# One level of Strassen's identity in the spatial product of a mixer kernel, with intermediates moved through DRAM

## The chip, the cores and the metric

The kernel runs on one core of a Trainium2 chip. The metric is the time of one execution on the device in microseconds (us). The core has a matrix engine (TensorE, PE in the profile, with its weight loads shown apart as PEld), VectorE (DVE), ScalarE (ACT), GpSimd (POOL) and SyncE (SP). PE multiplies a stationary 128x128 block by a moving block and adds into one of eight accumulator banks (PSUM); a bank holds 512 floats in each of 128 partitions. DMAs are issued from the queues of SP, ACT and POOL. Every engine takes its own instructions in the order of its program; engines wait for one another by semaphores.

## What is computed

`x` has 2048 rows (tokens) of 512. Two branches work on the normalized rows and are added to `x`.

```python
xn = layernorm(x)
# A: linear attention, 32 heads of 16
q, k, v = split(xn @ wqkv)
phi(t) = concat(softmax(t @ w_phi), softmax(-(t @ w_phi)))     # per head
o = phi(q) @ (phi(k)^T v) / (phi(q) . sum_s phi(k) + 1e-6)
A = o @ wo
# B: gated MLP, F = 1376, Fh = 688
z = gelu(xn @ w_in);  z1, z2 = z[:, :688], layernorm(z[:, 688:])
g = w_sp @ z2 + b_sp                    # 2048x2048 by 2048x688: the spatial product
B = (z1 * g) @ w_out
out = x + A + B
```

All data is 32-bit. A product that must keep precision is made from two parts of each operand, a rounded one (`h`, type fp32r) and the rest (`l`): h·h + h·l + l·h, three matmuls (`mm3`, L48). `round_h` (L39) makes h, mostly on ACT, and `rest_l` (L45) makes l on DVE.

## The kernel before, in words

The tokens are 16 tiles of 128 rows (`NT`); 688 is taken as two halves of 344 (`FC`). The statements are given in program order, but a scheduler of the framework orders the instructions of each engine by its own estimate of times, so parts of neighbouring stages interleave. Buffers come from pools; a tile that reuses a buffer waits for the last user of it.

**Projections (L145 to L301).** For each tile `s`: `center` subtracts the mean, transposes the tile on PE and splits it into `xT`; `proj_k`, `proj_q` and `proj_v` are 12 matmuls of 512 columns each; `softmax_pair` (L89) makes the two exponentials of k, their sums and reciprocals on DVE (maximum L92, minimum L93, two subtractions L95 and L96, sums L99, reciprocals L101) and ACT (L97). `proj_q` (L241) only scales the product on ACT and stores it to DRAM (`pq_d`). `add_kv` (L247) multiplies the exponentials by the reciprocals (L249), splits the product into kh and kl, adds it into `zacc` by an accumulating DMA on POOL's queue (L255) and adds to `kvps` with three fp32r matmuls of 256 columns for each of four head groups (L259). `z1_raw` (L122) makes the first half of the MLP input for 11 of the 16 tiles in this stage and stores it to DRAM (`z1_d`); the other five follow (L341).

**Second half of the MLP input (L366 to L386).** Per tile 24 matmuls of 344 columns (`zproj`), gelu on ACT, statistics on DVE (L376), the reciprocal deviation on POOL (`rstd_of`, L78), normalization on DVE (L382), and a split into `Z` (h and l) that stays on the chip. `kv_T` (L351) transposes and splits the attention state and broadcasts the sums of phi(k) into `zb`.

**Spatial product, attention and output together (L398 to L562).** For each output tile `i` and each of four quarters `q` of the 16 input tiles: `load_w` fetches a block of w_sp and splits it, two quarters ahead; `spatial` (L411) issues 4 x 6 matmuls of 344 columns into two banks. Around these stand, by hand: `q_prep` (L313), which loads the stored q product, runs `softmax_pair`, and makes phi(q) already divided by its denominator (multiplications by zb L319, sums L320, small operations L321 to L326, final product L328), stored by a DMA on SP's queue into an fp32r tile `er`; `attend` (L449), which for two tiles and one head group transposes er on PE (L454), splits (`fh`, `fl`), multiplies by the state (`po`) and splits again (`oT`); `gate` (L466), z1 times g plus bias; `gate_T` (L477), which transposes the gated tile on PE and splits it (`uh`, `ul`, `rt`); and `project` (L495), 29 matmuls of 512 columns with w_out and wo and the addition of x. So PE has matmuls of `spatial` to issue while the short chains of the other parts run.

Of the kernel before, what the change touches and what calls it, by code (L numbers as in the profile page):

```python
# [18 lines left out]
P = 128  # L19
S, D, H, DH, FH = 2048, 512, 32, 16, 688  # L20
NT = S // P
# [8 lines left out]
XB = 6  # L30
# [3 lines left out]
def mixer(ctx: ExitStack, tc: tile.TileContext, x, x_t, wv, wqkT, phi_bd, wo, w_in, wst, b_r, w_out, out):  # L34
# [4 lines left out]
    def round_h(eng, h, src):  # L39
        if eng is act:  # L40
            act.activation(h, src, AF.Copy)  # L41
        else:
            eng.tensor_copy(h, src)

    def rest_l(l, src, h, eng=None):  # L45
        (eng or dve).tensor_tensor(l, src, h.bitcast(F32), op=ALU.subtract)  # L46
# [14 lines left out]

    cst = ctx.enter_context(left("cst", 1))
    xz = ctx.enter_context(left("xz", NT))
    dram = ctx.enter_context(tc.tile_pool(name="dram", bufs=1, space=DRAM))
    pq_d = dram.tile([NT, P, D], F32, name="pq_d")
    z1_d = dram.tile([NT, P, FH], F32, name="z1_d")

# [21 lines left out]
    def softmax_pair(pl, src, tag, scale=1.0, ebufs=2):  # L89

        mm = pl.tile([P, 2, H], F32, tag=tag + "mm", bufs=2, name="mm")
        dve.tensor_reduce(mm[:, 0], heads(src), axis=AX.X, op=ALU.max)  # L92
        dve.tensor_reduce(mm[:, 1], heads(src), axis=AX.X, op=ALU.min)  # L93
        e = pl.tile([P, NF], F32, tag=tag + "e", bufs=ebufs, name="e")
        dve.tensor_tensor(heads(e[:, :D]), heads(src), bc(mm[:, 0], H), op=ALU.subtract)  # L95
        dve.tensor_tensor(heads(e[:, D:]), bc(mm[:, 1], H), heads(src), op=ALU.subtract)  # L96
        act.activation(e, e, AF.Exp, scale=scale)  # L97
        sm = pl.tile([P, 2 * H], F32, tag=tag + "sm", bufs=2, name="sm")
        dve.tensor_reduce(sm, heads(e), axis=AX.X, op=ALU.add)  # L99
        r = pl.tile([P, 2 * H], F32, tag=tag + "r", bufs=2, name="r")  # L100
        dve.reciprocal(r, sm)  # L101
        return e, r
# [4 lines left out]
    kvps = kv_ps_p.tile([P, NG, 2 * P], F32, name="kvps")  # L107
# [4 lines left out]
    def zproj(ps, s, w):  # L112
        p = ps.tile([P, 2, D], F32, tag="z", name="zps")
        t = xT[s]
        for j in range(2):
            for c in range(ND):
                cs = slice(c * P, (c + 1) * P)
                mm3(p[:, j, :FC], (t[:, 0, cs], t[:, 1, cs]), (w[j][0][:, c], w[j][1][:, c]),
# [19 lines left out]
    ones = w1_pool.tile([P, P], F32R, name="ones")  # L138
    ones_f = w1_pool.tile([P, P], F32, name="ones_f")
    pool.memset(ones_f, 1.0)  # L140
    dve.tensor_copy(ones, ones_f)
# [3 lines left out]
    with ExitStack() as p0:  # L145
# [42 lines left out]
        def load_win(dst, j, stp, bufs):  # L188
            for c in range(ND):
                t = stp.tile([P, D], F32, tag="x", bufs=bufs, name="wst_")  # L190
# [38 lines left out]
        def proj_v(s):  # L229
            pv = proj(s, wv_h, wv_l)  # L230
            vh = wk.tile([P, D], F32R, tag="vh", name="vh")
            vl = wk.tile([P, D], F32R, tag="vl", name="vl")
            r = r_x[:, s:s + 1]
            act.activation(vh, pv, AF.Copy, scale=r)
            dve.scalar_tensor_tensor(vl, pv, r, vh.bitcast(F32), op0=ALU.mult, op1=ALU.subtract)
            v[s] = vh, vl
# [4 lines left out]
        def proj_q(s):  # L241
            pq = proj(s, wqk_h[:, 0], wqk_l[:, 0])
            qs = wk.tile([P, D], F32, tag="qs", bufs=1, name="qs")
            act.activation(qs, pq, AF.Copy, scale=r_x[:, s:s + 1])
            act.dma_start(pq_d[s], qs)

        def add_kv(s, e, rs):  # L247
            vh, vl = v.pop(s)
            dve.tensor_tensor(heads(e), heads(e), bc(rs, 2 * H), op=ALU.mult)  # L249
            kh = wk.tile([P, 2, D], F32R, tag="kh", bufs=1, name="kh")  # L250
            kl = wk.tile([P, 2, D], F32R, tag="kl", bufs=1, name="kl")
            e2 = e.rearrange("p (a b) -> p a b", a=2)
            round_h(act, kh, e2)
            rest_l(kl, e2, kh)
            pool.dma_start(zacc, e, accum_op=ALU.add)  # L255
            for g in range(NG):
                gs = slice(g * P, (g + 1) * P)
                for i, (a, b) in enumerate(((vh, kh), (vh, kl), (vl, kh))):
                    pe.matmul(kvps[:, g], a[:, gs], b[:, :, gs],  # L259
                              start=(s == 0 and i == 0 and g % 2 == 0),  # L260
                              stop=(s == NT - 1 and i == 2), skip_group_check=True)
# [25 lines left out]
        n1 = 0  # L287
        for s in range(NT):
            fetch(s + 4)
            e, rs = ek if s == 0 else proj_k(s)  # L290
            if s + 2 < NT:
                center(s + 2)
            proj_q(s)
            add_kv(s, e, rs)
            if s + 2 < NT:
                proj_v(s + 2)
            if s in (0, 1):
                load_win(w1[s], s, wk, XB)
# [5 lines left out]
    Z = []  # L304
    ws = ctx.enter_context(right("ws", 2))
    cpre = ctx.enter_context(right("cpre", 1))
    kvT_h = cpre.tile([P, 2 * NG, P], F32R, name="kvT_h")
    kvT_l = cpre.tile([P, 2 * NG, P], F32R, name="kvT_l")
    zb = cpre.tile([P, NF], F32, name="zb")
    qp = ctx.enter_context(right("qp", 2))  # L310
    es = {}

    def q_prep(s):  # L313
        pq = qp.tile([P, D], F32, tag="pq", name="pq")
        sp.dma_start(pq, pq_d[s])
        e, r = softmax_pair(qp, pq, "q", ebufs=1)
        t = qp.tile([P, 2 * H], F32, tag="qt", name="qt")
        for a in range(2):
            dve.tensor_tensor(pq, e[:, a * D:(a + 1) * D], zb[:, a * D:(a + 1) * D], op=ALU.mult)  # L319
            dve.tensor_reduce(t[:, a * H:(a + 1) * H], heads(pq), axis=AX.X, op=ALU.add)  # L320
        dve.tensor_tensor(t, t, r, op=ALU.mult)  # L321
        den = qp.tile([P, H], F32, tag="den", name="den")
        dve.scalar_tensor_tensor(den, t[:, :H], EPS_DEN, t[:, H:], op0=ALU.add, op1=ALU.add)
        dve.reciprocal(den, den)
        w = qp.tile([P, 2 * H], F32, tag="qw", name="qw")
        dve.tensor_tensor(w.rearrange("p (a h) -> p a h", a=2), r.rearrange("p (a h) -> p a h", a=2),  # L326
                          den.unsqueeze(1).to_broadcast([P, 2, H]), op=ALU.mult)
        dve.tensor_tensor(heads(e), heads(e), bc(w, 2 * H), op=ALU.mult)  # L328

        er = qp.tile([P, NF], F32R, tag="er", name="er")  # L330
        sp.dma_start(er.bitcast(F32), e)
        return er
    with ExitStack() as p1:
        zw = p1.enter_context(left("zw", 2))
        w2_pool = p1.enter_context(left("w2", 1))
        w2 = [[w2_pool.tile([P, ND, FC], F32R, name=f"w2_{j}{k}") for k in "hl"] for j in range(2)]

        with psum("p1kv", 2) as psk, psum("zb", 1) as zbp:
            for j in range(2):
                load_win(w2[j], 2 + j, zw, 2)  # L340
            for s in range(NT - LAG, NT):  # L341
                z1_raw(zw, (za, zbp)[s % 2], s, 3)
            kvm = zw.tile([P, 2 * NG, P], F32, bufs=1, name="kvm")
            dve.tensor_tensor(kvm, kvps.rearrange("p g (a b) -> p (g a) b", a=2),
                              mask.unsqueeze(1).to_broadcast([P, 2 * NG, P]), op=ALU.mult)
            zh = zw.tile([P, NF], F32R, bufs=1, name="zh")
            zl = zw.tile([P, NF], F32R, bufs=1, name="zl")
            dve.tensor_copy(zh, zacc)
            rest_l(zl, zacc, zh)

            def kv_T():  # L351
                for k in range(2):
                    pt = psk.tile([P, NG, P], F32, tag="kvt", name="kvt")
                    for g in range(NG):
                        pe.transpose(pt[:, g], kvm[:, k * NG + g], ident)
                    dst = slice(k * NG, (k + 1) * NG)
                    round_h(act, kvT_h[:, dst], pt)
                    rest_l(kvT_l[:, dst], pt, kvT_h[:, dst])
                for k in range(2):
                    pz = psk.tile([P, D], F32, tag="kvt", name="pz")  # L360
                    cs = slice(k * D, (k + 1) * D)
                    pe.matmul(pz, ones, zh[:, cs], start=True, stop=False)
                    pe.matmul(pz, ones, zl[:, cs], start=False, stop=True)
                    dve.tensor_copy(zb[:, cs], pz)

            for s in range(NT):  # L366
                p = zproj((za, zbp)[s % 2], s, w2)
                if s == 2:
                    kv_T()
                if s in (4, 9):  # L370
                    es[s // 5] = q_prep(s // 5)
                z = zw.tile([P, 2, FC], F32, tag="zf", bufs=3, name="z2f")
                act.activation(z, p, AF.Gelu_apprx_tanh, scale=r_x[:, s:s + 1])
                st12 = zw.tile([P, 2, 6], F32, tag="st12", name="st12")
                for j in range(2):
                    dve.bn_stats(st12[:, j], z[:, j])  # L376
                mv = zw.tile([P, 2], F32, tag="mv", bufs=4, name="mv")
                r = zw.tile([P, 1], F32, tag="rstd", bufs=4, name="rstd")
                rstd_of(mv, r, st12.rearrange("p a b -> p (a b)"))
                m = mv[:, 0:1]  # L380
                zf = z.rearrange("p a b -> p (a b)")
                dve.tensor_scalar(zf, zf, m, r, op0=ALU.subtract, op1=ALU.mult)  # L382
                t = xz.tile([P, 2, FH], F32R, tag="xz", name="Z")
                round_h(act, t[:, 0], zf)
# [211 lines left out]
```

## Time and profile before

| | us |
|---|---|
| three runs shown | 707.5, 705.04, 705.25 |
| median | 705.25 |
| profiled execution | 704.55 |
| its span, first to last instruction | 702.8 |
| PE busy in it | 690.1 |
| DVE / ACT / POOL busy | 458.0 / 278.6 / 51.0 |
| granted PE clock | 1.0 |

The profiled execution is 1.75 us longer than its span (what lies around it). A group's row reads: line, engine, operation, output<-inputs, shapes, count | busy time of the group, mean duration of one in ns | idle time of the engine before it, and what ended it. Matmuls overlap in the records (a mean of 321 ns at a pace of about 157), so the pace is read from the starts of neighbours.

### The profile page before, as it was taken

Reading aid. Unit: us, or ns where it says so; the run is one execution under the profiler, and the core shown is the slowest. Engines: PE = TensorE matmul, PEld = TensorE weight load, DVE = VectorE, ACT = ScalarE, POOL = GpSimd, SP = SyncE. Lnnn points to the kernel's source line nnn. Section 1 sums busy time; section 2 is a strip of 40 time slices with the busy share of each in tenths; the row PEclk is TensorE's granted clock in tenths of the full one; section 3 lists DMA queues with packets and bytes.
Section 4 is the critical chain, followed back from the end, with each engine's and each line's share of the span. In section 5 each row is a group of like instructions: output and inputs, shape, how many; then the busy total and the mean of one; then the engine's idle time right before and its main releaser. Section 6 shows DMA issues by size and latency. Waiting matters only on the chain.

```text
span 702.8 us, 10333 instructions
## 1 busy us (share of the span) xinstructions
PE 690.1 (98%) x4092; PEld 641.3 (91%) x4092; DVE 458.0 (65%) x799; ACT 278.6 (40%) x418; POOL 51.0 (7%) x108
## 2 busy tenths in 40 slices
PE   6999999999999999999999999999999999999997
PEld 5888888889889999999999999999999999999996
DVE  5977775565665668975788778657667477373321
ACT  4654343343244445455334424344244343341210
POOL 2241111000000011310000000000000000000000
PEclk9999999999999999999999999999999999999999
DMA  8352533323236511125453433323333333233201
GB/s 299 126 126 75 125 96 96 81 80 92 69 100 169 178 36 46 46 73 175 133 167 120 146 120 111 110 95 106 111 105 128 101 113 110 96 125 90 62 0 46
DMA packets 35745, 75.27 MB, mean 107 GB/s; under 512 B 4112, under 2 KB 6160, under 8 KB 35696
## 3 DMA queue, kind: packets, MB, share of 16 engines
q1 hardware_dynamic: 28784, 56.38, 25.3%
q0 software_dynamic: 2304, 8.39, 6.4%
q10 hardware_dynamic: 4608, 9.83, 3.6%
q8 instruction: 32, 0.52, 0.3%
q14 instruction: 17, 0.14, 0.1%
HBM read 43.79 MB, written 14.02 MB: 82 GB/s over the span
## 4 chain that ended last, share of the span: by engine, by line
PE 95%; DMA 3%; ACT 1%; DVE 1%; issue 1%; SPq 0%; DVEq 0%; ACTq 0%
PE g L419 12%; PE g L423 12%; PE g L421 12%; PE proj L50 6%; PE proj L51 6%; PE proj L52 6%; PE zps L50 5%; PE zps L51 5%; PE zps L52 5%; PE pout L52 5%; PE pout L51 5%; PE pout L50 5%; PE kvps L259 3%; PE ptq L454 1%; PE po L50 1%; PE po L51 1%
## 5 line engine op out<-in xcount | busy, mean ns | idle before, releaser
L423 PE MATMUL g<-Z,wl 128*128 128x344 f32 x512 | 126.5, 321 | 0.0
L421 PE MATMUL g<-Z,wh 128*128 128x344 f32 x512 | 124.9, 321 | 0.0
L419 PE MATMUL g<-Z,wh 128*128 128x344 f32 x512 | 124.6, 322 | 0.0
L423 PEld LDWEIGHTS g<-Z,wl 128*128 128x128 f32 x512 | 89.2, 189 | 1.1
L419 PEld LDWEIGHTS g<-Z,wh 128*128 128x128 f32 x512 | 88.1, 188 | 2.2
L421 PEld LDWEIGHTS g<-Z,wh 128*128 128x128 f32 x512 | 88.4, 188 | 0.8
L41 ACT ACTIVATE wh<-wf 128x512 fp32r<-128x512 f32 x64 | 40.3, 629 | 103.6 <-PE g L421 64.0
L46 DVE TENSOR_TENSOR wl<-wf,wh 128x512 fp32r<-128x512 f32 x64 | 43.7, 685 | 27.8 <-ACT wh L41 27.2
L99 DVE TENSOR_REDUCE sm<-e 128x64 f32<-128x1024 f32 x32 | 38.9, 1216 | 29.7 <-ACT e L97 29.7
L50 PE MATMUL proj<-wqk_h,xT 128*128 128x512 f32 x128 | 51.2, 402 | 1.3 <-ACT wqk_h L41 1.3
L51 PE MATMUL proj<-wqk_l,xT 128*128 128x512 f32 x128 | 50.5, 394 | 0.0
L52 PE MATMUL proj<-wqk_h,xT 128*128 128x512 f32 x128 | 50.3, 393 | 0.0
L50 PE MATMUL zps<-w_0h,xT 128*128 128x344 f32 x128 | 41.4, 323 | 1.4 <-ACT z1f L124 1.4
L52 PE MATMUL zps<-w_0h,xT 128*128 128x344 f32 x128 | 40.9, 320 | 0.0
L51 PE MATMUL zps<-w_0l,xT 128*128 128x344 f32 x128 | 40.9, 320 | 0.0
L51 PE MATMUL zps<-w_1l,xT 128*128 128x344 f32 x128 | 40.9, 320 | 0.0
L52 PE MATMUL zps<-w_1h,xT 128*128 128x344 f32 x128 | 40.9, 320 | 0.0
L50 PE MATMUL zps<-w_1h,xT 128*128 128x344 f32 x128 | 40.9, 319 | 0.0
L92 DVE TENSOR_REDUCE mm<-proj 128x32 f32<-128x512 f32 x16 | 11.0, 690 | 33.2 <-PE proj L52 33.1
L46 DVE TENSOR_TENSOR kl<-e,kh 128x1024 fp32r<-128x1024 f32 x16 | 19.6, 1224 | 18.4 <-ACT kh L41 18.4
L50 PE MATMUL pout<-wu_h,uh 128*128 128x512 f32 x80 | 31.5, 394 | 0.0
L52 PE MATMUL pout<-wu_h,ul 128*128 128x512 f32 x80 | 31.3, 391 | 0.0
(182 smaller groups left out, 1508.4 us busy)
## 6 DMA issues: line engine op xcount, KB each, us to landing
wf<-in_wst SPq DMA_DIRECT2D x64, 256.0 KB, 3.2
zacc<-e POOLq DMA_DIRECT2D x16, 512.0 KB, 4.6
er<-e SPq DMA_DIRECT2D x16, 512.0 KB, 3.1
z_d<-z1f ACTq DMA_DIRECT2D x16, 344.0 KB, 3.6
z1t<-z_d SPq DMA_DIRECT2D x16, 344.0 KB, 3.6
xt<-in_x SPq DMA_DIRECT2D x16, 256.0 KB, 2.8
pq_d<-qs ACTq DMA_DIRECT2D x16, 256.0 KB, 2.0
pq<-pq_d SPq DMA_DIRECT2D x16, 256.0 KB, 3.1
```

The costliest lines, as they stand in the source:

```text
L41: act.activation(h, src, AF.Copy)
L46: (eng or dve).tensor_tensor(l, src, h.bitcast(F32), op=ALU.subtract)
L50: pe.matmul(dst, ah, bh, start=start, stop=False)
L51: pe.matmul(dst, ah, bl, start=False, stop=False)
L52: pe.matmul(dst, al, bh, start=False, stop=stop)
L92: dve.tensor_reduce(mm[:, 0], heads(src), axis=AX.X, op=ALU.max)
L99: dve.tensor_reduce(sm, heads(e), axis=AX.X, op=ALU.add)
L259: pe.matmul(kvps[:, g], a[:, gs], b[:, :, gs], start=(s == 0 and i == 0 and g % 2 == 0), stop=(s == NT - 1 and i == 2), skip_group_check=True)
L419: pe.matmul(g[:, j, :FC], h[:, c], z[:, 0, js[j]], start=first, stop=False)
L421: pe.matmul(g[:, j, :FC], h[:, c], z[:, 1, js[j]], start=False, stop=False)
L423: pe.matmul(g[:, j, :FC], l[:, c], z[:, 0, js[j]], start=False, stop=last)
L454: pe.transpose(pt[:, a, k].bitcast(F32R), es[k][:, a * D + g * P:a * D + (g + 1) * P], ident_r)
```

## The change

The spatial product takes pairs of output tiles, pairs of input tiles and the two halves of 688 as 2x2 blocks and forms each 2x2 block product from seven block products in place of eight (the variant of Strassen's identity with 15 additions). Two consecutive input tiles give B11, B12, B21, B22; two output tiles and two input tiles of w_sp give A11 to A22. The sums of B are made once, in the stage that makes z2 (`b_split`); the sums of A for each block of w_sp (`prep_a`); `products` issues 42 matmuls of 344 columns (7 products of 2 blocks of 3 matmuls) for each `n`, one of 32 steps (8 pairs of output tiles times 4 quarters); seven accumulators fill seven banks of an 8-bank pool, and `drain` combines them at the end of each pair of output tiles by one ACT copy and seven DVE additions of 344 columns, in the order of `FORM`. `load_z1` and the store of the gated tile in `gate` use POOL's queue.

```diff
+    def b_split(z, n):
+        tt = zw.tile([P, 4, FC], F32, tag="T", name="T")
+        dve.tensor_tensor(tt[:, 0:2], z[:, 1:3], z[:, 0:2], op=ALU.subtract)
...
+        b_parts(b11[:, 0, n % 2], b11[:, 1, n % 2], z[:, 0])
+        dve.tensor_tensor(tt[:, 2], z[:, 2], tt[:, 0], op=ALU.subtract)
...
+        b_parts(t[:, 0], t[:, 1], z[:, 2:4])
+        dve.tensor_tensor(tt[:, 3], z[:, 3], tt[:, 2], op=ALU.subtract)
...
+        b_parts(t[:, 0], t[:, 1], tt[:, 0:2])
...
+        b_parts(t[:, 0], t[:, 1], tt[:, 2:4])
...
+    def prep_a(n, f):
...
+        parts(("A11", "A12"), a)
+        dve.tensor_tensor(sums[:, 0], b[:, 0], b[:, 1], op=ALU.add)
+        dve.tensor_tensor(sums[:, 1], sums[:, 0], a[:, 0], op=ALU.subtract)
+        parts(("S1", "S2"), sums[:, 0:2])
+        dve.tensor_tensor(sums[:, 2], a[:, 0], b[:, 0], op=ALU.subtract)
+        dve.tensor_tensor(sums[:, 3], a[:, 1], sums[:, 1], op=ALU.subtract)
+        parts(("S3", "S4"), sums[:, 2:4])
+        parts(("A22",), b[:, 1:2])
+    FORM = (("P1", "A11", "B11"), ("P2", "A12", "B21"), ("P6", "S2", "T2"), ("P5", "S1", "T1"),
+            ("P7", "S3", "T3"), ("P3", "S4", "B22"), ("P4", "A22", "T4"))
+    def products(n, g):
...
+        for name, an, bn in FORM:
+            if n % NQ == 0:
+                g[name] = psg.tile([P, D], F32, tag="g", name="g")
+            for k in range(2):
+                (ah, al), (bh, bl) = ops[an], B[2 * q + k][bn]
+                mm3(dst, (ah[:, k], al[:, k]), (bh, bl), n % NQ == 0 and k == 0, n % NQ == NQ - 1 and k == 1)
...
+    for n in range(NC):
+        if n % NQ == 1:
+            z = load_z1(i)
+        products(n, g)
+        if n % NQ == NQ - 1 and i < NP - 1:
+            gate(i, drain(i, g), z)
...
+        if n + 3 < NC:
+            raw[n + 3] = load_a(n + 3)
+        if n + 2 < NC:
+            A[n + 2] = prep_a(n + 2, raw.pop(n + 2))
```

What else changes:

- `proj_q` runs `softmax_pair` on the product at once, about three tiles behind k, and stores exponentials and reciprocals (`e_d`, 544 KB per tile) by POOL's queue; `pq_d` goes. `q_fin` later loads them (SP), and does only the zb part: one product and one sum over 1024 elements, the small operations and the final product.
- `add_kv` keeps v and phi(k) in plain fp32: one fp32 matmul of 256 columns per head group in place of three fp32r ones; kh, kl and vl go. The sums of phi(k) are broadcast by two fp32 matmuls of 512 columns in place of four fp32r ones.
- In the z2 stage the normalization moves from DVE to ACT (`Identity` with bias and scale; a small POOL operation makes the bias); `Z` is replaced by 28 tiles of B parts, part of which take the buffers of `xT`. Four accumulator pools take turns in place of two. kvT and zb go to DRAM and are loaded again.
- The gated tiles go to DRAM (`u_d`) and are loaded as fp32r (SP), so that `gate_T` transposes fp32r.
- Attention and output no longer stand between the quarters of the spatial product but after it, as a last stage; phi(q) of a tile goes into its fp32r tile by POOL's queue in place of SP's (the first two tiles are transposed as plain fp32). For the last pair of output tiles the quarters are taken in the order 1, 2, 3, 0, and its drain follows the loads and splits of w_out and phi(q) of tile 0. `features` is `q_fin` and, from tile 2 on, the DMA into the fp32r tile:

```diff
+    for c in range(KF):
+        last = load_w(w_out, [(c * P, (c + 1) * P)], wu_h[:, c], wu_l[:, c])
...
+    done = features(0)
+    with tc.issue_after(last[0]), tc.issue_after(done):
+        cb = drain(NP - 1, g)
...
+    p = [project_u(i, gate_T(us.pop(i))) for i in range(2)]
...
+    oT, ins = attend_pair(0)
...
+    for i in range(NT):
+        if i < 2:
+            project_o(i, oT, p[i])
+        else:
+            nxt = gate_T(us.pop(i + 1)) if i + 1 < NT else None
+            project_o(i, oT, project_u(i, ut))
+            ut = nxt
...
+        for s in (2, 3) if i == 0 else (i + 3,):
+            if s < NT:
+                features(s)
...
+        if i % 2 and i + 1 < NT:
+            oT, _ = attend_pair(i + 1)
```

562 lines of the change are left out of this document (307 added, 255 removed).

## The prediction, made before the changed kernel ran

> **What bounds the kernel now.** I read the head of the page first, then the busy time by stretches of 20 us, then the chain of waits in a stretch of the spatial stage, then the groups by form for each engine, and last the landing times of the DMAs. The page, with busy us, share and count for each engine:
>
> ```profile
> span 702.8 us, 10333 instructions
> ...
> PE 690.1 (98%) x4092; PEld 641.3 (91%) x4092; DVE 458.0 (65%) x799; ACT 278.6 (40%) x418; POOL 51.0 (7%) x108
> ...
> PE 95%; DMA 3%; ACT 1%; DVE 1%; issue 1%; SPq 0%; DVEq 0%; ACTq 0%
> ```
>
> PE is busy for 690.1 of 702.8 us and carries 95% of the chain, so its list of work is the time, plus 12.7 us of idleness. Where that lies, by stretches (start:end length, busy us and count of PE, PEld, DVE, ACT, POOL, granted clock, DMA share, GB/s):
>
> ```profile
> 0.00:20.00 20.00, 13.13 (x67) 11.84 (x68) 11.98 (x23) 10.49 (x18) 6.32 (x21) 1.00 0.75 263
> 220.00:240.00 20.00, 18.58 (x122) 18.31 (x121) 12.07 (x18) 7.78 (x13) 0.86 (x1) 1.00 0.67 185
> 340.00:360.00 20.00, 20.00 (x123) 19.11 (x122) 19.27 (x35) 5.11 (x8) 0.00 (x0) 1.00 0.49 148
> 680.00:700.00 20.00, 18.74 (x95) 15.92 (x93) 3.79 (x8) 1.04 (x3) 0.00 (x0) 1.00 0.08 27
> ```
>
> The start costs 6.9 us, the hand-over between the two MLP stages 1.4, the end 1.3; nearly all of the rest lies after 700. From 340 to 360 DVE works 19.27 of 20 us and PE still 20.00: a dense DVE alone does not stop PE, because the short chains stand between matmuls that need nothing from them. The clock is full, so no gain can come from it. PE's paces, from the chain (start, us, what):
>
> ```profile
> 326.69 0.12 PE po L52
> 326.81 0.31 PE g L419 x2
> 327.12 0.31 PE g L421 x2
> 327.43 0.16 PE g L423
> 327.59 0.44 PE ptu L484 x4
> ...
> 328.30 0.23 PE pout L50
> ```
>
> ```profile
> 32.50 1.78 PE fold L180 x16
> ```
>
> ```profile
> 411.90 0.65 PE ptq L454 x8
> ```
>
> A matmul of 344 columns takes 0.157 us (0.31 for two, 0.16 for one), of 512 0.23, of 256 fp32r 0.12; an fp32 transpose takes 0.11 and an fp32r one 0.081 (0.65 / 8). `fold` multiplies plain fp32: 16 records are eight matmuls of 128 columns, 0.22 each.
>
> **PE's work.** The spatial product goes from 16 x 16 x 6 = 1536 matmuls to 32 x 42 = 1344: 192 x 0.157 = -30.2. In `add_kv`, 64 fp32 matmuls of 256 columns replace 192 fp32r ones. No row shows such an fp32 matmul; it lies between 0.22 (time independent of columns) and twice 0.22, and I take 0.44, since the fp32r matmuls do grow with columns: 64 x 0.44 - 192 x 0.12 = +5 (-9 at the other end, which would only help). The broadcast of the sums costs +0.9 by the same scaling. 96 transposes of gated tiles become fp32r: 96 x 0.029 = -2.8; 16 of phi(q) become fp32: +0.5. Sum: **-26.6**, if PE never waits more than now. The rest is what new idleness gives back.
>
> The DVE groups on which the waits rest (busy us, mean ns of one; the records overlap a little, so sums of means are upper bounds):
>
> ```profile
> L99 DVE TENSOR_REDUCE sm<-e 128x64 f32<-128x1024 f32 x32 | 38.9, 1216 | 29.7 <-ACT e L97 29.7
> L319 DVE TENSOR_TENSOR pq<-e,zb 128x512 f32<-128x512 f32 x32 | 21.8, 682 | 0.1
> L46 DVE TENSOR_TENSOR fl<-ptq,fh 128x512 fp32r<-128x512 f32 x32 | 21.8, 684 | 8.0 <-ACT fh L41 7.6
> L320 DVE TENSOR_REDUCE qt<-pq 128x32 f32<-128x512 f32 x32 | 21.0, 655 | 0.1
> L46 DVE TENSOR_TENSOR kl<-e,kh 128x1024 fp32r<-128x1024 f32 x16 | 19.6, 1224 | 18.4 <-ACT kh L41 18.4
> L249 DVE TENSOR_TENSOR e<-e,r 128x1024 f32<-128x1024 f32 x16 | 19.6, 1224 | 0.5
> L328 DVE TENSOR_TENSOR e<-e,qw 128x1024 f32<-128x1024 f32 x16 | 19.5, 1220 | 0.3
> L101 DVE RECIPROCAL r<-sm 128x64 f32<-128x64 f32 x32 | 17.4, 543 | 0.2
> L376 DVE BATCH_NORM_STATS2 st<-z2f 128x6 f32<-128x344 f32 x32 | 15.1, 505 | 4.5 <-ACT z2f L373 4.4
> L468 DVE SCALAR_TENSOR_TENSOR z1t<-g,bias,z1t 128x688 f32<-128x688 f32 x16 | 14.7, 917 | 15.3 <-PE g L423 15.3
> L46 DVE TENSOR_TENSOR Z<-z2f,Z 128x688 fp32r<-128x688 f32 x16 | 13.8, 863 | 1.5 <-ACT Z L41 1.4
> L46 DVE TENSOR_TENSOR oT<-po,oT 128x256 fp32r<-128x256 f32 x32 | 13.2, 414 | 15.2 <-ACT oT L41 15.1
> ...
> L324 DVE RECIPROCAL den<-den 128x32 f32<-128x32 f32 x16 | 5.6, 348 | 0.4
> L46 DVE TENSOR_TENSOR ul<-ptu,uh 128x128 fp32r<-128x128 f32 x16 | 4.6, 285 | 7.1 <-ACT uh L41 7.0
> ```
>
> ```profile
> L97 ACT ACTIVATE e<-e,r_x 128x1024 f32<-128x1024 f32 x16 | 18.4, 1149 | 18.9 <-DVE e L96 18.7
> ...
> L373 ACT ACTIVATE z2f<-zps,r_x 128x688 f32<-128x688 f32 x16 | 13.4, 836 | 21.3 <-PE zps L52 15.4 <-DVE Z L46 3.9 <-PE ptq L454 1.9
> ```
>
> **(a) Projections.** `kl` (1.22) and `vl` leave DVE; a q softmax comes: four operations of 512 elements, a sum (1.22) and a reciprocal (0.54), about 4.5 us. DVE then needs per tile about 12.7 us (k 5.7, q 5.5 since 16 tiles go into 13, stages of x 1.5), PE 13.85. DVE fits, but in its order 10 of 32 sums stand right behind their exponential (1.15 on ACT): up to 7 us in which it is idle. I take +2 of PE (0 to 8), because the margin of 1.1 us in each of 13 tiles covers most. ACT trades kh (as long as an exponential) and qs for the exponential. POOL's queue now holds the q stores behind `zacc`'s accumulations, which wait for `add_kv`; nothing on PE needs them soon.
>
> **(b) Hand-over to the z2 weights.** The loads of w_in stand behind two more stores on SP's queue: 2.0 where 1.4 is now, +0.6 (-0.4 to 3.6).
>
> **(c) From z2 into the spatial product.** Now the first spatial matmuls have Z of earlier tiles to work on. After the change, everything behind the last z2 matmul is one chain: gelu 0.84, statistics 2 x 0.5 and a combination 0.2, three small POOL operations, the normalization on ACT, seven DVE operations of the last B split (four of 688 elements, two of 344, one in between, 4.9), and, queued behind these on DVE, the first rest of block 1 of w_sp (0.68) which step 1 needs. A POOL operation:
>
> ```profile
> L81 POOL TENSOR_TENSOR rstd<-mv,mhalf 128x1 f32<-128x1 f32 x16 | 10.5, 657 | 1.3
> ```
>
> With 1.2 for POOL and 0.7 for the normalization that is 0.84 + 1.2 + 1.2 + 0.7 + 4.9 + 0.7 + hand-overs = 10.4. PE has step 0 meanwhile, 42 x 0.157 = 6.6. So +4 (0 to 8).
>
> **(d) Start of the last stage.** Nothing of it could be done on DVE ahead of the last drain except tile 0. From PE's last spatial matmul DVE does, in its order, until phi(q) of tile 3: the drain's end 0.9, nine operations of 1024 elements at 1.22 (11.0), the gate 1.6, twelve of 512 at 0.68 (8.2), four of 256 at 0.41, three of 128 and three reciprocals (1.9), eleven shorter ones at under 0.285 (2.4): at most 27.7, and with the overlap some 26.5. Then phi(q) goes by POOL's queue into its fp32r tile. The nearest DMAs (KB, median us to landing), and min/median/max of the first:
>
> ```profile
> zacc<-e POOLq DMA_DIRECT2D x16, 512.0 KB, 4.6
> er<-e SPq DMA_DIRECT2D x16, 512.0 KB, 3.1
> ```
>
> ```profile
> DMA to landing us min/median/max: 4.5/4.6/6.7
> ```
>
> I take 4.6, the same queue and size: 31 us behind the end of the spatial product. PE has before it needs tile 3's transposes: 75 matmuls of 512 (17.3), 24 of 256 (2.9), 18 fp32r and 16 fp32 transposes (3.3): 23.5. So **+7.5** (5 to 13). Behind the waiting transposes on PE stand the projections of the next two tiles; all engines wait for them.
>
> The Trainium skill ("DMA: Bandwidth & Descriptors", section "Anatomy of one DMA — SWDGE (gpsimd) path") gives for a DMA of POOL's queue about 2.0 us and the bytes at 436 GB/s. An estimate from that page is 3.2 us for 512 KB, where the accumulating row has 4.6; by it (d) would be 1.4 smaller.
>
> **(e) Rest of the last stage.** Each tile needs from DVE two products and a sum of 1024 (3.7), small operations (1.0), the rests of u (0.97) and the addition of x (0.69); each pair four rests of phi(q) and four of the attention (4.4): 2 x 6.3 + 4.4 = 17.0 us a pair; from PE 58 x 0.23 + 28 transposes x 0.081 + 24 x 0.12 = 18.5. PE is the longer, and phi(q) gets further ahead with each pair; the second pair comes about on time. **+4.5** (2 to 12).
>
> **(f) Spatial product.** Its steps need 42 x 0.157 = 6.6 us of PE and 4.1 of DVE (seven rests or splits of 0.68); with a drain and two gates a pair is 22 of 26.4 us. An accumulator's bank is drained in the order in which the next pair asks for it. +0.5 (0 to 3). The removed mixing of attention into this stage hid short chains; what is late next is (d) and (e).
>
> **Sum.** 2 + 0.6 + 4 + 7.5 + 4.5 + 0.5 = 19.1; -26.6 + 19.1 = -7.5. The profiled execution took 704.55, 0.7 below the median of 705.25: 704.55 - 7.5 = 697.05, **697**.
>
> **Rivals.**
>
> *A, the waits are hidden.* (a), (b), (e) and (f) near their low ends, (c) 1 and (d) 5: about 7 in all, 704.55 - 26.6 + 7 = **685** (680 to 689). For it speaks 20.00 beside 19.27 from 340 to 360; against it, that the work that covered the chains there now precedes them.
>
> *B, VectorE paces the last stage: slower.* The accumulators and buffers close a loop: the splits of a pair free DVE for the features of the next (13.9 in its order), then phi(q)'s DMA (up to 6.7), transposes 0.25 and a split on ACT 0.6: 21.5 against PE's 18.5. It decides as soon as that loop exceeds 18.5. Over seven pairs it costs 7 x 3 = 21 in place of (e), with (d) at 13: with 7.1 for (a), (b), (c) and (f) waits of 41, 704.55 - 26.6 + 41 = **719** (709 to 730). Against it: features of the next pair need nothing of the present one, so the loop may run open.
>
> *C, POOL's queue lands late.* If phi(q)'s DMAs land like the slowest row, 6.7 in place of 4.6, in the three early places where PE waits for them: +6.3, **703** (701 to 706).
> The Trainium skill ("SBUF — State Buffer", section "SBUF: two separate sides") says that GpSimd can't write the descriptors of its DMAs while a VectorE operation holds the port that the two share. The 6.7 among 4.6 may be such a case; no run so far shows it.
>
> That the spatial product does not shrink as told is no case with weight: the count of matmuls is in the code, and their shape has a row.
>
> **How the numbers follow.** Forecast 0.52 (own range 690 to 702), A 0.15, B 0.22, C 0.11. A measurement of this kernel tells about 0.5% (3.5 us) from no change. Below 701 to 701.7 (0.5% under the profiled execution and under the median) lie A and nearly all of the forecast, with a bit of C: 0.66; within 0.5% the rest of C and of the forecast: 0.12; above, B: 0.22. The range leaves out the lower part of A and the upper half of B, some 0.06 and 0.11: 684 to 718.
>
> **What would show it.** 1344 records of 344 columns at 0.157; 128 records in `add_kv` at about 0.22 each; PE idle some 4 us before spatial step 1, released by a DVE rest of w_sp; some 7.5 us about 24 us after the last spatial matmul, released by a phi(q) DMA; little idleness in later pairs. Idleness of 3 us in each later pair is B. I am wrong if PE waits inside the spatial steps, or if the projection stage idles over 8 us.

## The result, and the profile after

The changed kernel takes 694.66 us (median of 694.25 to 697.16) against 705.14 for the kernel before: a ratio of 0.985, interval 0.982 to 0.988. That is 10.5 us less; forecast were 697 us and a range of 684 to 718. The profiled execution of the changed kernel is the longest of the four, 697.16 with a span of 695.3, so its rows show 2.5 us more than the median.

The head of its page, busy time and chain:

```profile
span 695.3 us, 10319 instructions
...
PE 672.1 (97%) x3836; PEld 616.5 (89%) x3836; DVE 535.9 (77%) x972; ACT 279.4 (40%) x458; POOL 99.8 (14%) x186
...
PE 85%; issue 4%; POOL 4%; ACT 2%; DVE 2%; DMA 1%; SPq 0%; POOLq 0%; DVEq 0%; ACTq 0%
```

PE is busy 18.0 us less than before (690.1) and idle 23.2 us where it was 12.7. PE's share of the chain fell from 95% to 85%, and GpSimd (POOL), which had no part in it, now has 4%. What PE waited for (engine, line, releaser: us in all, times, longest):

```profile
PE g L50 <- ACT A L42: 3.7, 1, 3.7
PE g L50 <- ACT z L447: 2.3, 1, 2.3
PE proj L50 <- ACT wqk_h L42: 1.9, 1, 1.9
PE pout L52 <- DVE ul L46: 1.5, 1, 1.5
PE ptq L612 <- DMA er<-et: 1.2, 1, 1.2
```

The first two are the hand-over from z2 to the spatial product, the last two the start of the last stage. Nearly all of the rest of PE's idleness is the start of the program and its end. But 23.2 - 12.7 = 10.5 us of idleness and 26.6 us of saved matmuls would make 16 us less, and the span fell by 7.5. Most of the 8.6 us between them are in the clock. The hand-over in stretches of 2 us; the column behind POOL is the clock that PE was granted:

```profile
308.00:310.00 2.00, 1.70 (x11) 1.41 (x9) 1.45 (x4) 1.46 (x2) 0.37 (x2) 1.00 0.00 0
310.00:312.00 2.00, 0.03 (x1) 0.03 (x1) 2.00 (x5) 1.78 (x3) 1.33 (x2) 1.00 0.01 4
312.00:314.00 2.00, 2.00 (x9) 2.00 (x10) 1.73 (x4) 1.01 (x2) 0.82 (x2) 0.67 0.00 0
314.00:316.00 2.00, 2.00 (x9) 2.00 (x8) 1.49 (x4) 1.63 (x3) 0.80 (x1) 0.50 0.00 0
316.00:318.00 2.00, 2.00 (x14) 2.00 (x13) 0.62 (x2) 0.55 (x1) 1.23 (x3) 0.98 0.00 0
318.00:320.00 2.00, 1.44 (x10) 1.16 (x8) 1.55 (x2) 1.84 (x3) 0.00 (x0) 1.00 0.00 0
320.00:322.00 2.00, 0.00 (x0) 0.00 (x0) 2.00 (x5) 0.63 (x3) 0.00 (x0) 1.00 0.00 0
322.00:324.00 2.00, 0.84 (x3) 0.84 (x4) 1.49 (x3) 2.00 (x4) 1.19 (x2) 0.73 0.22 44
324.00:326.00 2.00, 2.00 (x9) 2.00 (x8) 2.00 (x6) 0.45 (x2) 0.00 (x0) 0.50 0.91 343
```

Behind each of the two gaps the clock is half for some 3.4 us, and PE, though "busy", does 9 matmuls in 2 us in place of 13. This execution has four such stretches (two here, two in the last stage) and a mean clock of 0.990, that is 0.010 x 695.3 = 7.0 us lost at the most (by the pace of the matmuls it is about 1.5 us for each stretch, 6.2 in all). The remaining 2 us lie in the last stage: PE's busy time there is 5.6 us above that of e12 below, where hardly a wait is left, and half clock is 3.4 of it at the most; what the rest is stays open. The three other executions had 0.995, 3.5 us lost, and spans of 692.4 to 693.1.

For the comparisons below I cut PE's timeline of each profiled execution at three places: the end of the last z2 matmul, of the last spatial matmul (each read from the start of the next matmul, since the records overlap), and of its last matmul of all.

| kernel | median us (ratio to before, interval) | spatial product | last stage |
|---|---|---|---|
| changed | 694.66 (0.982 to 0.988) | 221.2 | 161.8 |
| e1 block 1 early | 693.79 (0.982 to 0.986) | 214.0 | 163.1 |
| e2 useless matmuls | 693.23 (0.982 to 0.986) | 219.8 | 158.3 |
| e3 two tiles' splits first | 703.73 (0.996 to 0.999) | 221.3 | 169.0 |
| e4 e5 and e3 | 694.98 (0.984 to 0.987) | 212.2 | 167.7 |
| e5 block 1 early, gelu early | 691.40 (0.979 to 0.982) | 212.2 | 163.6 |
| e6 e5, features late | 718.71 (1.018 to 1.023) | 212.2 | 190.3 |
| e7 without features | 686.86 (0.973 to 0.976) | 222.1 | 151.4 |
| e8 eight products | 724.10 (1.026 to 1.029) | 250.8 | 158.9 |
| e9 fp32r state | 700.62 (0.993 to 0.995) | 221.8 | 159.2 |
| e10 e5, first split first | 692.58 (0.982 to 0.984) | 212.3 | 164.2 |
| e11 e10, rests on GpSimd | 693.59 (0.983 to 0.986) | 212.2 | 165.9 |
| e12 e5 and e7 | 677.93 (0.960 to 0.963) | 212.2 | 151.1 |

1344 matmuls at 0.157 are 211.0 us, so 212.2 is a spatial product with hardly a wait (0.5 us in e5 and e12).

### The profile page after: what moved, and what is told of

Read it like the earlier page. It is cut to its first block, busy times and chain, and to the rows that moved or that the text cites. A ratio compares the mean times of both kernels' runs of the same rounds, so it can differ in the third digit from the quotient of the medians.

```text
span 695.3 us, 10319 instructions
## 1 busy us (share of the span) xinstructions
PE 672.1 (97%) x3836; PEld 616.5 (89%) x3836; DVE 535.9 (77%) x972; ACT 279.4 (40%) x458; POOL 99.8 (14%) x186
## 4 chain that ended last, share of the span: by engine, by line
PE 85%; issue 4%; POOL 4%; ACT 2%; DVE 2%; DMA 1%; SPq 0%; POOLq 0%; DVEq 0%; ACTq 0%
PE g L50 10%; PE g L51 10%; PE g L52 10%; PE proj L50 6%; PE proj L52 6%; PE proj L51 6%; PE pout L52 5%; PE pout L50 5%; PE pout L51 4%; PE kvps L249 4%; PE zps L50 3%; PE zps L52 3%; PE zps L51 3%; POOL rstd L85 2%; POOL nb L455 1%
## 5 line engine op out<-in xcount | busy, mean ns | idle before, releaser
L50 PE MATMUL g<-B,A 128*128 128x344 f32 x448 | 144.9, 324 | 6.0 <-ACT A L42 3.7
L51 PE MATMUL g<-B,A 128*128 128x344 f32 x448 | 144.7, 323 | 0.0
L52 PE MATMUL g<-B,A 128*128 128x344 f32 x448 | 143.7, 321 | 0.0
L50 PEld LDWEIGHTS g<-B,A 128*128 128x128 f32 x448 | 85.4, 191 | 6.6 <-ACT A L42 4.0
L51 PEld LDWEIGHTS g<-B,A 128*128 128x128 f32 x448 | 85.4, 191 | 0.0
L52 PEld LDWEIGHTS g<-B,A 128*128 128x128 f32 x448 | 84.9, 190 | 0.0
L46 DVE TENSOR_TENSOR A<-S,A 128x512 fp32r<-128x512 f32 x64 | 44.0, 691 | 39.0 <-ACT A L42 38.2
L42 ACT ACTIVATE A<-S 128x512 fp32r<-128x512 f32 x64 | 40.2, 631 | 71.4 <-PE g L52 45.0
L102 ACT ACTIVATE e<-e,r_x 128x1024 f32<-128x1024 f32 x32 | 36.8, 1150 | 58.8 <-DVE e L101 58.2
L42 ACT ACTIVATE A<-wf 128x512 fp32r<-128x512 f32 x64 | 33.4, 523 | 38.6 <-PE g L52 38.6
L46 DVE TENSOR_TENSOR A<-wf,A 128x512 fp32r<-128x512 f32 x64 | 35.5, 555 | 3.2 <-ACT A L42 2.7
L42 ACT ACTIVATE fh<-ptq 128x512 fp32r<-128x512 f32 x32 | 18.2, 595 | 49.3 <-PE ptq L612 48.3
```

The source lines that it names most:

```text
L42: return act.activation(h, src, AF.Copy).ins
L46: return (eng or dve).tensor_tensor(l, src, h.bitcast(F32), op=ALU.subtract).ins
L50: pe.matmul(dst, ah, bh, start=start, stop=False)
L51: pe.matmul(dst, ah, bl, start=False, stop=False)
L52: pe.matmul(dst, al, bh, start=False, stop=stop)
```

## The experiments

My theory after the result: PE's list of work shrank by what was forecast, and 16 to 19 us of it were given back at just two places, the start of the spatial product and the start of the last stage, partly as idleness and partly as half clock behind it. Rivals were that the z2 stage or VectorE is late as a whole, so that each wait taken away comes back at the next, and that the half clock has another cause.

**e8, the size of the saving.** The seventh product is issued twice.

```diff
-                mm3(dst, (ah[:, k], al[:, k]), (bh, bl), ...)
+                for r in range(2 if name == "P4" else 1):
+                    mm3(dst, (ah[:, k], al[:, k]), (bh, bl), ...)
```

> The changed kernel with the seventh product issued twice, so that the spatial product has 1536 matmuls again, as many as in the kernel before (its result is counted twice, nothing else changes). Theory: PE bounds every step, 192 x 0.157 = 30.2 us more: 725 (723 to 727). Rival (another engine paces the steps, so that the saved matmuls were partly hidden anyway): less than 25 us more.

Measured: 724.10, 29.4 us more than the changed kernel; the spatial product grew by 29.6. The saved matmuls were worth their full pace, and nothing else paces the steps.

**e1, block 1 of w_sp early.** In the changed kernel its tiles took the place of z2's working tiles and so came behind the last use of these. Here the pool opens in the place that the z2 weights leave; drain and gate use z2's working tiles in its stead, and each gated tile is stored by two DMAs.

```diff
     ctx_w2.__exit__(None, None, None)
...
+    hl[1] = p2.enter_context(right("hl1", 1))
+    A[1] = prep_a(1, raw.pop(1))
     b_split(z2, NP - 1)
...
-    A[1] = prep_a(1, raw.pop(1))
```

> The splits of block 1 of w_sp get a place of their own (the one that the weights of z2 leave), and stand ahead of the last B split on ACT and DVE. Theory (a stall at the start of the spatial product, and behind each stall a stretch in which the granted clock is half): the idle 3.71 us ahead of step 1 goes, the 2.27 us ahead of the second product stays; with the half-speed stretch behind it, 1.8 us, some 4 to 5.5 us less than the changed kernel: about 690. Rival 1 (the whole z2 stage is late, by GpSimd and ACT, and PE only waits at another place): the idleness comes back at step 2 or 3, under 1 us less. Rival 2 (the half clock has nothing to do with the idleness): the stretch of half clock after 320 stays, 3.7 us less.

Measured: the gap ahead of step 1 is gone and did not come back at step 2 or 3; the spatial product takes 7.2 us less. That refutes the first rival's reason. But the whole kernel gained only 0.9 in the median (5 in the profiled execution), which misses the forecast of about 690 and is the time that this rival had: the last stage's order on DVE shifted, and PE waits 3.2 us on rests of phi(q) there that it had not waited for. The three executions that were not profiled also have a clock of 0.987 to 0.991, where those of the changed kernel have 0.995, so that a part of the gain went into half clock.

**e2, the clock.** PE is given useless work in the second gap.

```diff
+        if n == 1:
...
+            with tc.issue_after(step):
+                for k in range(22):
+                    ins = pe.matmul(fill[:, :FC], ident_r, B[0]["B11"][0], start=k == 0, stop=k == 21).ins
```

> The changed kernel with 22 extra matmuls of 344 columns into the unused eighth bank between step 0 and step 1 of the spatial product: 22 x 0.157 = 3.45 us of useless work in the place of the 3.71 us of idleness; the output is the same. Theory (idleness makes the clock fall): the wait for block 1 ends at the same time, but PE goes on at full clock after it: in the profile no half clock between 320 and 328, up to 1.8 us less. Rival (the half clock has another cause): the half clock stays there and the time is the same, or longer if the extra work delays anything.

The same stretches of this kernel as those of the changed kernel above:

```profile
320.00:322.00 2.00, 1.59 (x11) 1.30 (x9) 2.00 (x5) 0.69 (x2) 0.00 (x0) 1.00 0.00 0
322.00:324.00 2.00, 0.59 (x4) 0.59 (x5) 1.49 (x4) 1.94 (x4) 1.19 (x2) 1.00 0.12 19
324.00:326.00 2.00, 2.00 (x14) 2.00 (x14) 2.00 (x5) 0.71 (x2) 0.00 (x0) 1.00 0.91 319
326.00:328.00 2.00, 2.00 (x15) 2.00 (x14) 1.32 (x4) 0.26 (x1) 0.00 (x0) 1.00 0.77 241
```

The clock stays at 1.00 and PE does 14 matmuls from 324 to 326 in place of 9. The profiled execution has a mean clock of 1.000, the four have 0.995 to 1.000, and the median is 1.4 us under the changed kernel's, though the intervals overlap. More work made the kernel no slower. But this one execution can't tell the fill from chance, for behind the first gap, which was left as it was, the clock stayed full too. That idleness makes the clock fall is shown by the kernels together: in all their traces each of the 26 stretches at half clock, up to PE's last matmul, begins within a wait of PE of 1.2 us or more or some 2.4 us behind one at the latest; e6 below, with the most waits, has a clock of 0.970 to 0.978, and e12, with none of that length behind the start, 0.999 to 1.000 in all its executions.

**e5, both gaps gone.** As e1, and the last but one B split is held back on ACT until the gelu of the last z2 tile, whose accumulator the second product waited for.

```diff
+        if s == NT - 1:
+            with tc.issue_after(last_gelu):
+                b_split(zlast, s // 2 - 1)
```

> Block 1 of w_sp early and the gelu of the last z2 tile ahead of the last but one B split; the last stage's program as in the changed kernel. Theory: from the end of z2's matmuls to the end of the spatial product PE takes 212 us in place of 221.2, as in the run that had both, and the last stage stays at 161.8 +- 2: a span of 684 to 688, 686 to 690 in all. Rival (VectorE's chain, not PE, sets the start of the last stage, and its order shifts with every edit): the last stage grows by 3 to 6 and the time stays at 690 to 694.

Measured: the spatial product is at 212.2 as forecast, 9.0 us less, but the last stage grew by 1.8 and the time is 691.4: 3.3 us under the changed kernel's median, and the shortest of the kernels that leave nothing out. It is a miss of 1.4 us beyond the theory's range, on the rival's side: some of what is gained ahead of the last stage is waited for in it, and all of its half clock (5.1 us by the granted clock, 3.4 in the changed kernel's last stage) lies there.

**e3, e4 and e10, the order in the last stage.** In e3 the splits of the first two gated tiles stand ahead of the features of tile 1; e4 adds that to e5; e10 moves only those of the first tile.

```diff
-        features(1)
...
-    p = [project_u(i, gate_T(us.pop(i))) for i in range(2)]
...
+    u01 = [gate_T(us.pop(i)) for i in range(2)]
+    with tc.issue_after(lasts[1]):
+        features(1)
+    p = [project_u(i, u01[i]) for i in range(2)]
```

> In the last stage, the splits of the first two gated tiles stand on DVE right behind the drain, ahead of the features of tile 1 and the small w_out rows. Theory: PE's idle 1.54 us on the rest of the gated tile shrinks to about 0.5, and the stretch of half clock behind it (1.8 us) goes; the features of tile 3 come about 1 us later, so that the wait for its phi(q) grows by about 2 us with the PE time saved: 0 to 2 us less in all. Rival (VectorE paces the last stage as a whole): no change, each wait that goes comes back in full at the next.

> Block 1 of w_sp early, the gelu of the last z2 tile ahead of the last but one B split on ACT, and the splits of the first gated tiles first. Theory: both waits between z2 and the spatial product go (6.0 us idle, 3.6 us at half clock lost) and 0 to 2 us of the last stage: 684 to 688. Rival (the z2 stage is late as a whole): over 690.

> The version with block 1 early and the earlier gelu, and in the last stage only the splits of the very first gated tile moved on DVE right behind the drain. Theory (the order in which VectorE works off the first 30 us is the bound of that stretch): PE's 1.5 us on the first rest goes, phi(q) of tile 3 comes 0 to 1 us later: 0 to 2 us less than that version, 688 to 692. If the features fall back as they did when both tiles' splits were moved, it is slower, up to 697.

Measured: e3 is 9 us slower than the changed kernel. The 1.5 us wait for `ul` went, and PE waited 6.2 us for phi(q) of tile 3 in place of 1.2; by the granted clock its last stage also loses 8.5 us to half clock where the changed kernel's loses 3.4. e4 (695.0, forecast 684 to 688) lost in the last stage what it gained ahead of it (167.7 us). e10 is level with e5 and just over its range. So my theory fell for this place. The first 30 us of the last stage in the changed kernel and in e3:

```profile
529.80:559.80 30.00, 26.49 (x138) 21.10 (x135) 28.80 (x52) 8.85 (x22) 2.17 (x4) 0.94 0.64 241
```

```profile
529.26:559.26 30.00, 26.04 (x127) 21.22 (x125) 24.17 (x45) 8.98 (x22) 0.53 (x1) 0.89 0.57 198
```

In the changed kernel VectorE works 28.8 of these 30 us, so its whole list paces them, and none of these orders has shortened them; e7 below takes work from the list, and the waits go. The order of e3 also made VectorE itself wait (24.2 us of work), which fits its being slower and not just level.

**e7, without the features.** `q_fin`'s operations are left out.

```diff
-            e, ins = q_fin(cw, ets.pop(s), zb)
+            e, ins = ets[s][:, :NF], dve.reciprocal(ets[s][:, NF:], ets[s][:, NF:]).ins
```

> The changed kernel with the three long DVE operations and the small ones of each tile's features left out in the last stage (phi(q) is stored as it was loaded, without sums and denominators; one small operation stays). DVE has 4.6 us less per tile. Theory (waits only at the start of the stage): the last stage goes from 161.8 us to about 152, since some 5.3 us of idleness and 3.5 us at half clock go: about 685 in all. Rival (DVE paces the whole stage): much more than 9 us less, down to PE's bare 148 us. If under 4 us go, the waits are of loads, not of DVE.

Measured: 686.86, 7.8 less; the last stage takes 151.4, 10.4 us less, the price of this work of DVE (5.0 us of it idleness of PE, 3.4 half clock by the granted clock, 2.0 that I can't place), while the spatial product took 0.9 longer in this execution.

**e6, features late.** As e5, and from the second pair on features stand behind the rests of phi(q) of the present pair.

```diff
-        rest_l(fl, pt, fh)
+        lasts[2] = rest_l(fl, pt, fh)
...
-        for s in (2, 3) if i == 0 else (i + 3,):
-            if s < NT:
-                features(s)
+        if i == 0:
+            features(2)
+            features(3)
+        if i % 2 == 0 and i > 0 and i + 3 < NT:
+            features(i + 3)
...
         if i % 2 and i + 1 < NT:
-            oT, _ = attend_pair(i + 1)
+            oT, ins = attend_pair(i + 1)
+            if i + 3 < NT:
+                with tc.issue_after(lasts[2]):
+                    features(i + 3)
```

> As the run before, and from the second pair on the features of later tiles stand on DVE behind the splits of phi(q) of the present pair. Theory (the waits of the last stage are a matter of what stands ahead of fl, ul and phi(q) of tile 3 in DVE's order, not of DVE's total): 2 to 4 us less than the run before, 683 to 687. Rival (DVE's total paces the whole stage): no gain, and 1 to 3 us of idleness in each later pair.

Measured: 718.71, 27 us slower than e5. The rival's idleness came, but with a loss that neither theory had: 16.2 us of waits and some 11 of clock (a mean of 0.978 in place of 0.993). PE's waits, and two of the six, one pair apart:

```profile
PE ptq L619 <- DMA er<-et: 16.2, 6, 3.6
```

```profile
575.70 0.54 PE L619 MATMUL ptq<-ident_r,er 128*128 128x128 f32 x4 [3.14 <-DMA er<-et]
```

```profile
598.89 0.28 PE L619 MATMUL ptq<-ident_r,er 128*128 128x128 f32 x1 [2.07 <-DMA er<-et]
```

A pair takes 23.2 us, and DVE has idle time in it too (5.2 us ahead of 576.9). This is the loop of rival B: rests, features, store, transposes, rests. It costs nothing while features run ahead, and paces the stage when they don't.

**e9, the state in fp32r again.** kh, kl, vh, vl return; for their room the tiles of x have three buffers in place of five.

```diff
+            round_h(act, kh, e)
+            rest_l(kl, e, kh)
...
+                pe.matmul(kvps[:, g], vh[:, gs], kh[:, :, gs], start=first, stop=False, skip_group_check=True)
+                pe.matmul(kvps[:, g], vl[:, gs], kh[:, :, gs], start=False, stop=False, skip_group_check=True)
+                pe.matmul(kvps[:, g], vh[:, gs], kl[:, :, gs], start=False, stop=last, skip_group_check=True)
```

> The changed kernel with v and phi(k) split again (one ACT copy of 1024 and two DVE rests of 1024 and 512 more per tile, three buffers of x in place of five), and three fp32r matmuls of 256 columns per head group in place of one fp32. Theory (PE bounds the projections only as long as DVE's 12.7 us per tile stay under PE's 13.9): PE's work falls by 4.7 us, but DVE needs 14.7 us per tile against PE's 13.5: PE idles over 1 us in each of 13 tiles, 5 to 15 us more in all than the changed kernel. Rival (VectorE is not near the bound there): 4 to 5 us less.

Measured: 700.62, 6.0 slower, at the low end of the forecast. Two stretches of the projections, full in the changed kernel:

```profile
40.00:60.00 20.00, 15.80 (x82) 13.52 (x81) 17.21 (x28) 9.60 (x14) 2.80 (x5) 0.91 0.54 128
...
220.00:240.00 20.00, 18.28 (x113) 17.17 (x112) 17.19 (x23) 7.47 (x8) 2.84 (x4) 1.00 0.52 138
```

PE loses 4.2 and 1.7 us in them, and in the first some clock. The idleness does not come in every tile, as I had it, so the step of 1.2 us per tile was too simple. What ended these four waits was ACT's rounding of phi(k) twice (3.2 and 1.0), once DVE's rest of x (1.0) and once ACT's copy of z1 (0.7), so the loss is not VectorE's alone, and the part of the fewer buffers is not shown.

**e11, rests on GpSimd.** As e10, with five rests of weights on GpSimd.

```diff
-        return round_h(act, h, t[:rows]), rest_l(l, t[:rows], h)
+        return round_h(act, h, t[:rows]), rest_l(l, t[:rows], h, eng)
```

> As the run before, and five rests of weights (the small w_out rows and the four blocks of wo, 0.68 us each on DVE) go to GpSimd. Theory: 3.4 us of DVE's work go from its fullest stretch, and phi(q) of tile 3 comes that much earlier: 2 to 5 us less than the run before, 684 to 689. Rival (GpSimd is slow beside a busy VectorE, as some of its small operations were in the z2 stage, or its queue holds up the phi(q) stores behind the rests): no gain or a loss.

Measured: 693.59, no gain. While GpSimd works at its four rests, VectorE's operations get slower; in the changed kernel these took 0.21, 0.19, 0.23 and 1.22. The four together take 3.4 us more here, as much as the five rests had cost VectorE:

```profile
531.98 4.96 POOL L46 TENSOR_TENSOR wol<-wof,woh 128x512 fp32r<-128x512 f32 x4 [5.37 <-DMA xr<-in_x]
```

```profile
532.24 1.11 DVE L316 TENSOR_TENSOR qt<-qt,et 128x64 f32<-128x64 f32 x1
533.39 1.16 DVE L318 SCALAR_TENSOR_TENSOR den<-qt 128x32 f32<-128x32 f32 x1
...
534.97 0.84 DVE L321 TENSOR_TENSOR qw<-et,den 128x64 f32<-128x64 f32 x1
535.84 2.18 DVE L323 TENSOR_TENSOR et<-et,qw 128x1024 f32<-128x1024 f32 x1
```

**e12, both places at once.** e5 and e7 together.

> Both places relieved at once: block 1 early and the earlier gelu, and the DVE work of the features left out in the last stage (phi(q) is stored as it was loaded). Theory (what PE saved went to just these two places, as idleness and as half clock behind it): the two gains add, 694.7 - 9 - 7.8 = 678, which is also the kernel before less the 26.6 us of matmuls: 676 to 681, with the granted clock at 1.0. Rival (there is a third place): over 683.

Measured: 677.93, with a granted clock of 0.999 to 1.000 in all four executions.

```profile
span 676.7 us, 10253 instructions
...
PE 663.4 (98%) x3836; PEld 611.5 (90%) x3836; DVE 475.6 (70%) x876; ACT 278.6 (41%) x458; POOL 107.8 (16%) x202
```

PE is busy 663.4 us: 690.1 - 26.7. By stages the two gains add, 9.0 us in the spatial product (as in e5) and 10.7 in the last stage (10.4 in e7), and there is no third place. In the medians they do more than add: 16.7 us, where e5 has 3.3 and e7 7.8, since with one place relieved PE still waits at the other. The forecast of 678 took 9 from a stage of the profile and 7.8 from medians, so that it hit this well is in part luck.

## Why the prediction was right, point by point

The time came out 2.3 us under the forecast, by the mechanism that was forecast; inside the sum some terms are off.

**PE's work, -26.6.** Right. e12 shows -26.7, e8 29.4 of the 30.2 for the spatial product. The fp32 matmul of 256 columns, which no row of before showed, takes 0.43 (four matmuls, eight records):

```profile
62.43 1.73 PE kvps L249 x8
```

**(a), projections, +2.** It was 0: PE is never idle between 40 us and the end of the z2 stage. e9 shows how near the margin was: with 2 us more of DVE and a rounding more of ACT per tile, and fewer buffers, the whole is 6.0 longer, although PE's work was to be 4.7 shorter.

**(b), +0.6.** It was -1.4: the idleness at the z2 weights is gone altogether.

**(c), from z2 into the spatial product, +4.** Mis-sized: 9.0 (e5 against the changed kernel), beyond my upper end of 8. The wait that I had forecast, some 4 us ahead of step 1, came with 3.7, though ACT's rounding of w_sp ended it and not DVE's rest. Beside it came one of 2.3 inside step 0, and half clock behind both. A wait inside a spatial step was my own sign of being wrong, and at this place I was. The chain behind the last z2 matmul took 14.5 us (308.6 to 323.1) in place of 10.4. ACT's rows show how it began late:

```profile
308.51 0.96 ACT L456 ACTIVATE z<-z,nb,rstd 128x688 f32<-128x688 f32 x1 [0.64 <-POOL nb L455]
...
311.10 0.82 ACT L447 ACTIVATE z<-zps,r_x 128x688 f32<-128x688 f32 x1
...
317.45 0.96 ACT L456 ACTIVATE z<-z,nb,rstd 128x688 f32<-128x688 f32 x1 [1.82 <-POOL nb L455]
...
322.49 0.61 ACT L42 ACTIVATE A<-wf 128x512 fp32r<-128x512 f32 x1
```

The last gelu could begin at about 308.7 and stood behind a normalization that waited for GpSimd and two splits: 2.4 us. From its end at 311.9 to its normalization at 317.45 it is 5.5 us, where I had 2.4 for the statistics and GpSimd: DVE did other work of B ahead of the statistics and of their combination, and GpSimd's three operations took 2.0 in place of 1.2. I had taken the chain as if its engines were free. The second thing missed is that the spatial product's second accumulator is the one that this gelu reads. The third is the half clock, for which I had no term: I wrote that the clock is full, so that no gain can come from it, and did not ask what it would do behind a gap.

**(d), start of the last stage, +7.5.** The chain was right and the wait was elsewhere. T, the end of PE's last spatial matmul, is 529.8. The last product of tile 3's features, and the transposes that wait for it:

```profile
555.20 1.22 DVE L323 TENSOR_TENSOR et<-et,qw 128x1024 f32<-128x1024 f32 x1
```

```profile
559.96 0.78 PE L612 MATMUL ptq<-ident_r,er 128*128 128x128 f32 x7 [1.25 <-DMA er<-et]
```

phi(q) was done on DVE at T + 26.6 (forecast 26.5) and there at T + 30.2 (31). PE waited only 1.25, since it came at T + 28.9 in place of T + 23.5: it had already lost 2.3 us waiting for the drain and the rests of the first gated tile, which stood behind tile 1's first product on DVE, and some 1.7 to half clock; 1.4 of its delay I can't place.

**(d) and (e) together, 12.** e7 gives 161.8 - 151.4 = 10.4. From 600 us to the end of its work PE is idle for 0.15 us, so the later pairs wait even less than (e) had it.

**(f), 0.5.** It was 0. The DVE work of a step is 4.2 us in eight rests and sums, as I had it (4.1), but not as I had written it: seven of 0.68 would be 4.8.

**The sum of the waits, 19.1.** The profiled spans of the changed kernel and of e12 are 18.6 apart, the medians 16.7. That the sum fits better than its parts is luck: (a), (b), (e) and (f) were too high and (c) too low. And I had summed waits alone, while in the profiled execution PE's idleness grew by 10.5 and up to 7.0 more was half clock, a term that I had left out.

**The rivals.** A: the waits were not hidden; if all are, the time is 678 (e12), not 685. B: its loop exists, and e6 that closes it comes to 718.7 where B was priced at 719, if from other parts (a loop of 23.2 in place of 21.5, and the clock); in the change's own order it stays open. C: in the changed kernel phi(q)'s DMAs landed as fast as the faster of the two rows of before, not as the slowest:

```profile
er<-et POOLq DMA_DIRECT2D x14, 512.0 KB, 3.0
```

The 3.0 is near the 3.2 us that I estimated in the prediction from the Trainium skill ("DMA: Bandwidth & Descriptors", section "Anatomy of one DMA — SWDGE (gpsimd) path"), so for this kernel that estimate was the better one, and the accumulating DMA, which I took, the slower case. It is no fixed time, though: in e7 and e12, where no features stand between these DMAs, their medians are 4.9 and 4.4 us and the slowest takes 8.3.

## What to carry to other kernels

Taking matmuls away from a kernel bound by TensorE is worth their full pace, but the chains of the other engines that they covered come into view at the ends of stages: add up, per stage, what each engine must do between the last matmul of one stage and the first of the next, with the queue that it already has. To a wait of TensorE of 3 us or more add the half clock behind it, here about 1.5 us for each stretch of 3.4; behind waits of 1.2 to 3 us it may come or not. And where two engines feed each other around a loop, the lead between them is what keeps it free: an order that spends the lead costs more than the operations that it moves.

## What the runs showed of the hardware

- **Behind idleness TensorE's clock can be halved.** After gaps of 2.27 and 3.71 us matmuls of 344 columns start 0.286 us apart in place of 0.157, for 3.4 us each time, about 1.5 us lost. The same gap of 2.27 us cost no clock in the profiled executions of e1 and e2, while a gap of 1.25 us among short ones did in the last stage of the changed kernel: the length of such a gap alone does not decide, and executions of one kernel differ by it (mean clock 0.990 and 0.995). Behind every wait of 3 us or more in the traces of this case, the start of the program apart, the clock was half for at least 3.4 us (behind those of 5.3 and 7.7 us in e7 and e9 for 6.8). The Trainium skill ("TensorE: Matmul & The Clock Gate", section "HAM oscillation — how this bites in real kernels") tells of such a fall behind idle gaps of over about 3.4 us; here the stretch at half clock has that length, but shorter gaps were enough.
- **Beside each other, VectorE and GpSimd are slower.** The small GpSimd operation that makes the bias of the normalization takes 0.27 us at least and at the median and 1.66 at most, while VectorE was at work, and VectorE's operations of 0.2 us took up to 1.16 beside GpSimd's rests in e11. The Trainium skill's rule cited with rival C ("SBUF — State Buffer", section "SBUF: two separate sides") lets one of the two block the other; both rows agree with it, and no late phi(q) store showed it. The row of that small operation (minimum, median and maximum in ns):

```profile
L455 POOL TENSOR_SCALAR nb<-mv,rstd x16: 267/268/1659, 259.3 to 317.2; 128x1 f32<-128x1 f32 x16
```
